# Folding the last heads of a two-layer Hedgehog and Mish kernel in chunks of six, four and four, and making the output weights' parts one by one

## The chip, the cores and the metric

The kernel runs on one core of one Trainium2 chip. The time of a run is the device time in microseconds (us), and lower is better. The engines are called as in the profile: PE is the TensorE's matmuls and PEld its weight loads, DVE the VectorE, ACT the ScalarE, POOL the GpSimd and SP the SyncE, which here only issues DMA.

## The reference

All arrays are float32: x is (1, 2048, 640), wqkv (640, 1920), w_phi (32, 20, 20), wo (640, 640), w1 (640, 1536), w2 (1536, 640). There are 32 heads of 20 columns. The two halves are run twice, with the same weights, so there are two layers.

```
def attention(x, wqkv, w_phi, wo):               # x is layer-normalised
    q, k, v = split per head of x @ wqkv
    pq = q @ w_phi[h];  pk = k @ w_phi[h]        # per head, 20 x 20
    phi_q = concat(softmax(pq), softmax(-pq));  phi_k = the same of pk
    kv = phi_k^T v;  z = sum of phi_k over the sequence
    o = (phi_q @ kv) / (phi_q @ z + 1e-6)
    return concat of heads(o) @ wo

def dense(x, w1, b1, w2):                        # x is layer-normalised
    h = x @ w1 + b1
    return mish(h) @ w2

x = x + attention(norm(x));  x = x + dense(norm(x))
x = x + attention(norm(x));  x = x + dense(norm(x))
```

## The kernel before

**Stages.** Each layer is three stages: `attend_first` (keys, queries and values, and the sum over the sequence), `attend_second` (the averages, the product with wo and the residual) and `dense`. In each the 2048 rows go through in 8 blocks (`NB`) of two tiles (`BT`) of 128 rows, which the text counts from 0. Layer 0's first stage ends at about 263 us of the profiled span; its second and third stages end at about 707, where layer 1 begins.

**Split matmuls.** Every large product is made of three float32r products: each operand is split into a high part (an ACT copy that rounds) and a low part (operand minus high part). So x comes as `xth` and `xtl`, a weight as `r1h`/`r1l` (the wide set of keys and values, later w1) or `r2h`/`r2l` (queries, later wo and w2). `Transposed.step` turns a normalised block on the TensorE (L280), copies it to `xth` on ACT and subtracts on DVE (L286) for `xtl`.

**Folding.** The per-head w_phi is folded into the query and key weights in layer 0 only. The host lays w_phi out as blocks on a diagonal, `phi_bd` (120 x 6 x 120): column group t holds heads 6t to 6t+5, and group 5 holds only heads 30 and 31, 40 rows. `load_raw` fetches the transposed weights wqk_t in the same chunks: five of 120 rows and a sixth of 40. `fold_phi` then makes each of the five 128-row parts `k` of the folded weight in two halves `c`: three matmuls (L237) of float32, one for each chunk, that write side by side into one PSUM tile. The first half covers heads 0 to 17 (360 columns), the second heads 18 to 31 (280 columns: 120, 120 and 40). An ACT copy gives the high part and a DVE subtraction (L243) the low part. The order of the ten halves is that of the tuple in `fold_phi`: first halves of parts 0 to 3, second halves of parts 0 to 3, then both of part 4. The queries are folded at the start, before and among the first projections (L344); the keys at about 36 to 47 us, just before the first key tile of block 0. After block 1 of layer 0 the folded weights are written out (`spill_qk_weights`), and layer 1 reads them back.

**Start.** The first DMAs stand in an order written out by hand (`manual_schedule` for SP, L448 on): the first three groups of `phi_bd`, three query chunks, x of block 0, the other three groups of `phi_bd`, three query chunks, then the weights of the values and the key chunks. The sixth chunk lies in a wide weight tile (`r2_wide`) and the other five in the future places of `r2` tiles.

**Output weights.** wo is made into five parts by the generator `make_five`: at its first step it fetches three parts (L149's raw), and at each later step it makes one part, an ACT copy (L148) and a POOL subtraction (L149), and in the first two of these it fetches one part more. The five fetches land in places of weight tiles not yet used and, the fifth, in a row tile (`row_tile`, a pool of 4 that also holds the normalised rows `xn`). `load_o_weights` runs the whole generator at once, at the end of block 1 of the first stage, in both layers.

**Order.** Within a block of the first stage, `order` gives the sequence of projections (keys, queries, values of the two tiles). Each is a generator: `features` takes a projection through the two softmaxes (reductions, reciprocals and products on DVE and POOL: L368 to L379), and a later step adds its key product to `kva` (L416). The next block's x is fetched and turned in the course of the block. Outside the hand-written part at the start, a scheduler that simulates the timeline sets each engine's order, except that ACT's instructions in `act` and those within `issue_after` keep to a named predecessor. `attend_second` fixes the order of TensorE and SP by hand.

Of the kernel before, what the change touches and what calls it, by code (L numbers as in the profile page):

```python
# [41 lines left out]
def kernel(  # L42
# [77 lines left out]
    def v_tile():  # L120
        return work.tile([P, VW], F32, tag="v", name="v", bufs=2)
# [80 lines left out]
                raws.append(fetch_rows(rows(3 + k), [spares[3 + k]()]))  # L202
            yield w

    def load_o_weights():
        return list(make_five(KD, lambda k: wo[k * P:(k + 1) * P, :]))[1:]

    def w2_pair(f):

        return r2_pair(f if f < 5 else (f + 5 if f < 7 else f - 2))  # L210
# [1 line left out]
    def load_raw(which, ts=range(6)):  # L212

        raw = []
        for t in ts:
            rows = 120 if t < 5 else 40
            if t < 5:
                r = wts.tile([P, D], F32, tag=f"r2{'hl'[which]}{5 + t}", name=f"raw{which}{t}")
            else:
                r = r2_wide(10 + which, F32)[:, 0]  # L220

            n = P if t < 5 else rows
            nc.sync.dma_start(r[:n], wqk_t[which * D + t * 120:which * D + t * 120 + n, :])
            raw.append((r, rows))
        return raw

    def fold_phi(ws, bd, raw):

        pss = {}
        for k, c in ((0, 0), (1, 0), (2, 0), (3, 0), (0, 1), (1, 1), (2, 1), (3, 1), (4, 0), (4, 1)):  # L230
            if c == 0:
                mm = None if k % 2 else mm_tile()
                pss[k] = [one_tile(), one_tile()] if k % 2 else [mm[:, 0], mm[:, 1]]
            ps = pss[k][c]
            for t in range(3 * c, 3 * c + 3):
                r, rows = raw[t]
                nc.tensor.matmul(ps[:, (t % 3) * 120:(t % 3) * 120 + rows],  # L237
                                 r[:rows, k * P:(k + 1) * P], bd[:rows, t, :rows],
                                 start=True, stop=True)
            n0, n1 = (0, 360) if c == 0 else (360, D)  # L240
            hi, lo = ws[k][0][:, n0:n1], ws[k][1][:, n0:n1]
            nc.scalar.activation(hi, ps[:, :n1 - n0], AF.Copy)
            nc.vector.tensor_tensor(lo, ps[:, :n1 - n0], hi.bitcast(F32), op=ALU.subtract)  # L243
# [143 lines left out]
    def attend_first(layer, x_src, first):  # L387


        def fetch_normed(b):  # L390
            if layer:
                return load_turned(n2_d[b], [row_tile] * 3)
            xt = fetch(x_src, b)
            norm_scale(b, [norm_stats(t, xt) for t in range(BT)])
            return xt

        pending = []

        def advance():
            for g in pending[::-1]:  # L400
                try:
                    next(g)
                except StopIteration:
                    pending.remove(g)

        def keys(xts, i, v):
            e = big_tile()
            yield from features(project(xts, i % BT, kv_ws, 0), e, False)
            yield
            if i % BT == 0 and BT < i < NT - BT:  # L410
                yield
            for r in range(9):
                for j in range(4):
                    h = 3 * (4 * (r // 3) + j) + r % 3
                    if h < H:
                        nc.tensor.matmul(kva[32 * j:32 * j + DH + 1, 40 * r:40 * r + 40],  # L416
                                         v[:, (DH + 1) * h:(DH + 1) * (h + 1)], e[:, 40 * h:40 * h + 40],
                                         start=(i == 0 and r == 0), stop=(i == NT - 1), skip_group_check=True)

        def queries(xts, i, ps=None):  # L420
            e = query_tile(i)
            yield from features(project(xts, i % BT, q_ws, 0) if ps is None else ps, e, True)

            nc.vector.transpose(e, e)
            b, t = divmod(i, BT)
            dst = e_d[b].rearrange("(j f) (t q s) -> t q f j s", f=32, t=BT, s=32)
            for q in range(4):
                nc.sync.dma_start(dst[t, q], e[32 * q:32 * q + 32].rearrange("f (j s) -> f j s", s=32))
                if b == NB - 1:
                    yield  # L430

        def values(xts, i, v):
            vv = v.rearrange("p (h d) -> p h d", d=DH + 1)
            act(vv[:, :, DH], ident[:, :H], AF.Copy, scale=0.0, bias=1.0)
            if i < BT:
                pv = project(xts, i, kv_ws, D, [one_tile(), one_tile()])
                for c in range(2):
                    act(vv[:, c * H // 2:(c + 1) * H // 2, :DH],
                        pv[c][:, :HC].rearrange("p (h d) -> p h d", d=DH), AF.Copy)
            else:  # L440
                pv = project(xts, i % BT, kv_ws, D)
                act(vv[:, :, :DH].rearrange("p (c h) d -> p c h d", c=2),
                    both(pv).rearrange("p c (h d) -> p c h d", d=DH), AF.Copy)
            yield

        if first is None:
            with tc.manual_schedule(engines={mybir.EngineType.SP}):
                bd = big_tile()[:120, :720].rearrange("p (t c) -> p t c", t=6)  # L448
                nc.sync.dma_start(bd[:, :3], phi_bd[:, :3])
                raw = load_raw(0, range(3))  # L450
                xt = fetch_normed(0)
                nc.sync.dma_start(bd[:, 3:], phi_bd[:, 3:])
                raw += load_raw(0, range(3, 6))
                nxt = normed(0, xt).all()
                q_ws = [r2_pair(k) for k in range(KD)]
                fold_phi(q_ws, bd, raw)
                kv_ws = load_v_weights()
                raw = load_raw(1)
            nc.sync.dma_start(mask, bass.AP(tensor=head_mask.tensor, offset=head_mask.offset,
                                            ap=[[1, 120], [120 * (DH + 1), 3]]))  # L460
        else:
            nxt, kv_ws = first
            load_k_weights(kv_ws)
            q_ws = load_q_weights()
        for b in range(NB):
            xts = nxt
            order = ("k0", "k1", "v0", "v1", "q0", "q1")
            if b == 0 and layer:
                order = ("v0", "k0", "k1", "v1", "q0", "q1")
            elif b == 0:  # L470
                order = ("v0", "q0", "v1", "k0", "q1", "k1")
            elif b == 1 and not layer:
                order = ("k0", "q0", "k1", "v0", "q1", "v1")
            elif b == NB - 1:
                order = ("k0", "k1", "v0", "v1", "q0")
            vs = [v_tile() for _ in range(BT)]
            for n, (kind, t) in enumerate(order):
                t = int(t)
                i = b * BT + t
                if b == 0 and n == (1 if layer else 3):  # L480
                    if layer == 0:
                        fold_phi(kv_ws, bd, raw)
                    kva = one_tile()
                    nc.vector.memset(kva[:, :360], 0.0)
                if b == NB - 1 and n == 3:
                    loaded = {0: load(0)}
                if b + 1 < NB:
                    if n == 0:
                        xt = fetch_normed(b + 1)
                    elif n == 2:  # L490
                        nxt = xt if layer else normed(b + 1, xt)
                    elif n > 2:
                        nxt.step()
                g = {"k": lambda: keys(xts, i, vs[t]), "q": lambda: queries(xts, i),
                     "v": lambda: values(xts, i, vs[t])}[kind]()
                next(g)
                advance()
                pending.append(g)
            if b == 1:
                if layer == 0:  # L500
                    spill_qk_weights(kv_ws, q_ws)
                o_ws = load_o_weights()

        def rest():

            ps = [one_tile(), one_tile()]
            project_half(ps[0], xts, 1, q_ws, 0, 0)
            advance()
            advance()
            yield  # L510
            project_half(ps[1], xts, 1, q_ws, 0, 1, range(3))
            yield
            project_half(ps[1], xts, 1, q_ws, 0, 1, range(3, KD))
            pending.append(queries(xts, NT - 1, ps))
            next(pending[-1])
            while pending:
                yield
                advance()

        return kva, o_ws, loaded, rest()  # L520
# [374 lines left out]
```

## Time and profile before

| what | value |
|---|---|
| median of 3 runs | 1381.55 us (1381.36 to 1382.13) |
| profiled execution | 1381.04 us, its span 1379.0 |
| granted TensorE clock | 0.999 |
| PE busy | 1364.3 us, 99% |
| DVE busy | 1077.0 us, 78% |
| ACT busy | 583.3 us, 42% |
| POOL busy | 441.0 us, 32% |
| DMA queue of the kernel's transfers | 45.0% of 16 engines' span |

The span is the time from the first to the last instruction of the profiled execution; 2.0 us of the time lie outside of it. A busy share is a sum over the whole span and says little of one stage: in the 40 slices of the page the DMA is at 8 tenths in the first slice and at 2 to 7 later, DVE is at 9 tenths in the third to fifth slice (69 to 172 us, inside layer 0's first stage) and mostly at 6 to 8 elsewhere, and PE is at 9 in all slices but the first, where it has 7, and the last, where it has 8. In a timeline a line gives the start, the length and the engine, then the line of the code, the operation, output and input tiles by their names, their shape, and how many such instructions in a row; idle time before it stands in brackets, with what ended it. Instructions of a row overlap their neighbours, so that the distance of two starts, and not the length, is what one costs.

### The profile page before, as it was taken

To read this page: it belongs to the slowest core of one execution; us is meant where nothing else is said; L and a number is where in the kernel's file an instruction comes from. 1 tells how busy PE (TensorE), PEld (TensorE's weight loads), DVE (VectorE), ACT (ScalarE), POOL (GpSimd) and SP (SyncE) were. 2 spreads that over 40 slices of the span, in tenths; PEclk is the share of its full clock that TensorE was granted. 3 is DMA by queue.
4 is the path that set the end of the run, shared out by engine and by line. 5 is a ranking of instruction groups with operands and counts; after the bars stand their busy time and mean duration, and the time that the engine had idled before them with its cause. 6 is when DMAs were issued, how large, how long until landed. Compare 5 with 4: busy or idle time off the path is not lost.

```text
span 1379.0 us, 30804 instructions
## 1 busy us (share of the span) xinstructions
PE 1364.3 (99%) x12866; PEld 1350.7 (98%) x12866; DVE 1077.0 (78%) x1820; ACT 583.3 (42%) x971; POOL 441.0 (32%) x334
## 2 busy tenths in 40 slices
PE   7999999999999999999999999999999999999998
PEld 7999999999999999999999999999999999999998
DVE  5799977886698887788769898988668776677775
ACT  4444434222355444545454333432235444354443
POOL 1353543353322221222234434453342111111112
PEclk9999999999999999999999999999999999999999
DMA  8532433779624533344473433458965321333200
GB/s 321 173 67 62 73 54 61 211 227 316 227 68 96 115 90 62 80 116 96 117 262 74 95 59 59 70 117 274 297 239 163 77 53 45 97 96 96 77 20 19
DMA packets 350277, 169.67 MB, mean 123 GB/s; under 512 B 287098, under 2 KB 323690, under 8 KB 350138
## 3 DMA queue, kind: packets, MB, share of 16 engines
q1 hardware_dynamic: 350137, 167.72, 45.0%
q8 instruction: 100, 1.64, 0.5%
q14 instruction: 40, 0.32, 0.1%
HBM read 104.76 MB, written 62.91 MB: 122 GB/s over the span
## 4 chain that ended last, share of the span: by engine, by line
PE 94%; DVE 2%; DMA 1%; issue 1%; POOL 0%; SPq 0%; ACT 0%; DVEq 0%; POOLq 0%; ACTq 0%
PE mm L344 26%; PE one L691 24%; PE mm L733 24%; PE one L344 12%; PE mm L569 3%; PE one L280 2%; PE one L416 2%; PE mm L237 1%; DMA raw<-in_wqk_t 1%; DVE m L368 1%; PE one L237 0%; DMA v<-in_wv 0%; DVE big L371 0%; DVE r L377 0%; DMA raw<-in_wo 0%
## 5 line engine op out<-in xcount | busy, mean ns | idle before, releaser
L733 PE MATMUL mm<-r2h,ol 128*128 128x320 f32 x1280 | 305.0, 309 | 0.3 <-ACT ol L716 0.3
L717 POOL TENSOR_TENSOR ol<-big,ol 128x512 fp32r<-128x512 f32 (+1 forms) x98 | 130.4, 1330 | 483.6 <-ACT ol L716 407.4
L691 PE MATMUL one<-xtl,r1h 128*128 128x256 f32 x960 | 268.2, 279 | 0.0
L691 PE MATMUL one<-xth,r1l 128*128 128x256 f32 x960 | 268.0, 279 | 0.0
L691 PE MATMUL one<-xth,r1h 128*128 128x256 f32 x960 | 265.9, 279 | 0.0
L733 PEld LDWEIGHTS mm<-r2h,ol 128*128 128x128 f32 x1280 | 219.2, 188 | 0.6 <-ACT ol L716 0.6
L733 PE MATMUL mm<-r2l,ol 128*128 128x320 f32 x640 | 197.3, 309 | 0.0
L344 PE MATMUL mm<-r1h,xth 128*128 128x320 f32 x600 | 187.5, 312 | 0.0
L344 PE MATMUL mm<-r1h,xtl 128*128 128x320 f32 x600 | 185.8, 310 | 0.4 <-DVE xtl L286 0.4
L344 PE MATMUL mm<-r1l,xth 128*128 128x320 f32 x600 | 186.0, 310 | 0.0
L691 PEld LDWEIGHTS one<-xtl,r1h 128*128 128x128 f32 x960 | 180.4, 188 | 0.0
L691 PEld LDWEIGHTS one<-xth,r1l 128*128 128x128 f32 x960 | 180.4, 188 | 0.0
L691 PEld LDWEIGHTS one<-xth,r1h 128*128 128x128 f32 x960 | 179.6, 188 | 0.0
L706 DVE TENSOR_SCALAR big<-big 128x512 f32<-128x512 f32 (+1 forms) x98 | 56.4, 575 | 110.6 <-ACT big L704 110.4
L379 POOL TENSOR_TENSOR r<-r,r 128x1280 f32<-128x1280 f32 x32 | 76.6, 2395 | 154.3 <-DVE r L378 148.5
L733 PEld LDWEIGHTS mm<-r2l,ol 128*128 128x128 f32 x640 | 120.2, 188 | 0.0
L708 ACT ACTIVATE big<-big,two 128x512 f32<-128x512 f32 (+1 forms) x98 | 70.3, 717 | 116.0 <-DVE big L707 116.0
L704 ACT ACTIVATE big<-one,b1s 128x256 f32<-128x256 f32 x192 | 81.0, 468 | 90.1 <-PE one L691 89.6
L716 ACT ACTIVATE ol<-big 128x512 fp32r<-128x512 f32 (+1 forms) x98 | 61.0, 623 | 136.3 <-DVE big L715 136.2
L344 PEld LDWEIGHTS mm<-r1h,xth 128*128 128x128 f32 x600 | 112.7, 188 | 0.8
L344 PEld LDWEIGHTS mm<-r1h,xtl 128*128 128x128 f32 x600 | 112.7, 188 | 0.7 <-DVE xtl L286 0.6
L344 PEld LDWEIGHTS mm<-r1l,xth 128*128 128x128 f32 x600 | 112.8, 188 | 0.1
(128 smaller groups left out, 3124.0 us busy)
## 6 DMA issues: line engine op xcount, KB each, us to landing
e_d<-r SPq DMA_DIRECT2D x128, 160.0 KB, 4.0
big<-e_d SPq DMA_DIRECT2D x32, 640.0 KB, 7.3
x_d<-xt SPq DMA_DIRECT2D x23, 640.0 KB, 3.6
xt<-x_d SPq DMA_DIRECT2D x22, 640.0 KB, 4.4
n_d<-xn SPq DMA_DIRECT2D x176, 80.0 KB, 2.3
xt<-in_x SPq DMA_DIRECT2D x16, 640.0 KB, 6.8
xn<-x_d SPq DMA_DIRECT2D x28, 320.0 KB, 4.4
v<-n_d SPq DMA_DIRECT2D x30, 256.0 KB, 3.1
```

The source lines that it names most:

```text
L280: nc.tensor.transpose(ps[:, c, t * P:(t + 1) * P], self.rows[t][:, (c0 + c) * P:(c0 + c + 1) * P], ident)
L344: nc.tensor.matmul(ps[:, :HC], a[:, sl], r, start=(k == 0 and n == 0), stop=(k == KD - 1 and n == 2))
L379: nc.gpsimd.tensor_tensor(eg, eg, r.unsqueeze(2).to_broadcast([P, 2 * H, DH]), op=ALU.mult)
L416: nc.tensor.matmul(kva[32 * j:32 * j + DH + 1, 40 * r:40 * r + 40], v[:, (DH + 1) * h:(DH + 1) * (h + 1)], e[:, 40 * h:40 * h + 40], start ...
L569: nc.tensor.matmul(po[64 * q:64 * q + 64, c, GW * j:GW * j + w], phs[g][:n, s0:s0 + 64], kvb[:n, g, :w], start=True, stop=True)
L691: nc.tensor.matmul(ph[:, j, :], l, r, start=(n == 0), stop=(n == 3 * KD - 1))
L704: exps[0] = nc.scalar.activation(part(ta, 0)[:, j - js.start], ph[:, j, :], AF.Exp, bias=b1s[:, 2 * pr + j:2 * pr + j + 1]).ins
L706: nc.vector.tensor_scalar_min(e, e, E_CAP)
L708: nc.scalar.activation(r, n, AF.Ln, bias=two)
L716: nc.scalar.activation(ah[:, js], n, AF.Copy)
L717: nc.gpsimd.tensor_tensor(al[:, js], n, ah[:, js].bitcast(F32), op=ALU.subtract)
L733: nc.tensor.matmul(pys[t][:, c, :HC], l[:, j, sl], r, start=(f == 0 and n == 0), stop=(f == KF - 1 and n == 2))
```

## The change

The last fourteen heads are folded in chunks of six, four and four heads (120, 80 and 80 rows), where they were folded in chunks of six, six and two (120, 120 and 40). For this `phi_bd` stays as it is in memory; group 4 is fetched as before and only its first 80 rows and columns are used, and group 5 is put together in place, from the last two heads of group 4 and the two of group 5, by two DMAs of 40 x 40 elements onto a memset area. The sixth chunk of raw weights is the last 80 rows.

The parts of wo are no longer all made at the end of block 1. There only the three first fetches are issued; one part is then made at the beginning of each of blocks 2 to 6, ordered after the last of ACT's instructions so far. This holds in both layers.

```diff
-    def load_o_weights():
-        return list(make_five(KD, lambda k: wo[k * P:(k + 1) * P, :]))[1:]
...
     def load_raw(which, ts=range(6)):
         for t in ts:
-            rows = 120 if t < 5 else 40
+            rows = 120 if t < 4 else 80
...
             n = P if t < 5 else rows
-            nc.sync.dma_start(r[:n], wqk_t[which * D + t * 120:which * D + t * 120 + n, :])
+            c0 = which * D + (t * 120 if t < 5 else D - rows)
+            nc.sync.dma_start(r[:n], wqk_t[c0:c0 + n, :])
...
     def fold_phi(ws, bd, raw):
...
+            n = 0
             for t in range(3 * c, 3 * c + 3):
                 r, rows = raw[t]
-                nc.tensor.matmul(ps[:, (t % 3) * 120:(t % 3) * 120 + rows],
-                                 r[:rows, k * P:(k + 1) * P], bd[:rows, t, :rows],
+                nc.tensor.matmul(ps[:, n:n + rows], r[:rows, k * P:(k + 1) * P], bd[:rows, t, :rows],
                                  start=True, stop=True)
+                n += rows
...
                 xt = fetch_normed(0)
-                nc.sync.dma_start(bd[:, 3:], phi_bd[:, 3:])
+
+                nc.vector.memset(bd[:80, 5, :80], 0.0)
+                nc.sync.dma_start(bd[:40, 5, :40], phi_bd[80:120, 4, 80:120])
+                nc.sync.dma_start(bd[40:80, 5, 40:80], phi_bd[:40, 5, :40])
+                nc.sync.dma_start(bd[:, 3:5], phi_bd[:, 3:5])
                 raw += load_raw(0, range(3, 6))
...
             vs = [v_tile() for _ in range(BT)]
+            if 2 <= b < 2 + KD:
+                with tc.issue_after(last_act[0]):
+                    o_ws.append(next(o_gen))
...
             if b == 1:
                 if layer == 0:
                     spill_qk_weights(kv_ws, q_ws)
-                o_ws = load_o_weights()
+                o_gen = make_five(KD, lambda k: wo[k * P:(k + 1) * P, :])
+                next(o_gen)
+                o_ws = []
```

## The prediction

> **What bounds the kernel now.** I read the page first, then the waits of the TensorE over the whole span, then the timeline of each place that the diff touches.
>
> ```profile
> PE 1364.3 (99%) x12866; PEld 1350.7 (98%) x12866; DVE 1077.0 (78%) x1820; ACT 583.3 (42%) x971; POOL 441.0 (32%) x334
> ...
> PE 94%; DVE 2%; DMA 1%; issue 1%; POOL 0%; SPq 0%; ACT 0%; DVEq 0%; POOLq 0%; ACTq 0%
> ```
>
> ```profile
> PE mm L237 <- DMA raw<-in_wqk_t: 7.9, 3, 4.4
> ...
> PE mm L344 <- DVE xtl L286: 0.4, 1, 0.4
> ...
> PE mm L237 <- DVE r1l L243: 0.2, 1, 0.2
> ```
>
> The TensorE is busy throughout and the chain that ends last is 94% TensorE. So only two things can save time: TensorE work that goes away, and the few places where it waits. Both lie in layer 0's first stage, up to 91.4 us. Layer 1 folds nothing and has no such wait in its first stage, so there the change can only cost.
>
> Next the timeline of the weight loads in the key folding (columns: start, length from the first to the last end, engine, line, operation, tiles, shape, count). L237 is the folding's matmul, and each of them takes two passes, each with a weight load of its own.
>
> ```profile
> 36.26 0.75 PEld L237 LDWEIGHTS one<-big,raw 120*128 120x128 f32 x6
> 36.93 0.75 PEld L237 LDWEIGHTS mm<-big,raw 120*128 120x128 f32 x6
> 37.60 1.20 PEld L237 LDWEIGHTS one<-big,raw 120*128 120x128 f32 x10
> 38.91 0.29 PEld L237 LDWEIGHTS one<-big,r 40*128 40x128 f32 x2
> 39.25 0.52 PEld L237 LDWEIGHTS one<-big,raw 120*128 120x128 f32 x4
> 39.88 0.29 PEld L237 LDWEIGHTS one<-big,r 40*128 40x128 f32 x2
> 40.23 0.52 PEld L237 LDWEIGHTS mm<-big,raw 120*128 120x128 f32 x4
> ```
>
> Six passes of 120 rows take 0.67 us (36.26 to 36.93). Six passes of which the last two have 40 rows take 0.98 (39.25 to 40.23), though 40 columns fewer go through. The time is lost at the change of row count: four passes to 39.88 take 0.64, not 0.45, and two passes of 40 rows take 0.34, not 0.22. Whether 80 rows are spared this, the same view of the second stage's averages (L569) shows:
>
> ```profile
> 264.40 1.25 PEld L569 LDWEIGHTS mm<-kvb,big 120*64 120x64 f32 x40 [0.19 <-DVE kvb L543]
> 265.56 0.20 PEld L569 LDWEIGHTS mm<-kvb,ol 80*64 80x64 f32 x4
> 265.68 1.25 PEld L569 LDWEIGHTS mm<-kvb,big 120*64 120x64 f32 x40
> ```
>
> 40 loads in 1.16 us and 4 in 0.12 are 0.029 each: going from 120 to 80 rows and back costs nothing.
>
> Last, the two waits that are not DMA, in the timelines of POOL, DVE and the TensorE:
>
> ```profile
> 44.07 1.58 POOL L149 TENSOR_TENSOR r2l<-raw,r2h 128x640 fp32r<-128x640 f32 x1 [0.56 <-PE mm L237]
> ...
> 44.12 1.61 DVE L262 SCALAR_TENSOR_TENSOR stats<-mv,stats 128x1 f32<-128x1 f32 x2
> ...
> 90.95 0.35 DVE L286 TENSOR_TENSOR xtl<-one,xth 128x256 fp32r<-128x256 f32 x1
> ...
> 91.36 0.41 PE L344 MATMUL mm<-r1h,xtl 128*128 128x320 f32 x1 [0.42 <-DVE xtl L286]
> ```
>
> Two tiny DVE instructions (0.23 together at 28.53) take 1.61 while POOL subtracts an output-weight part, and the subtraction behind them (45.65) is what the TensorE waits for at 46.23. At 91.36 it waits for the last split of block 2, out of a DVE that has been busy without a gap since 60.
>
> **Query folding.** Its second halves lose 0.31 each, at 20.39, 22.25 and 25.72; the two earlier ones, whose 40-row passes stand together at 13.32, run at 0.213 per pass and lose about 0.4 in all. That 0.4 is not kept: at 18.84 and 19.75 the TensorE waits for DVE, whose run starts when block 1's x lands (14.29) and reaches the first split at 19.70. That transfer moves. An issue on SP waits for the eighth one before it, and the two added issues put x of block 1 behind block 0's x: it goes out at 9.5, not 6.39. Bytes ahead of it: 102 KB more for 80 rows, 58 less for the band's two groups, 13 for the two small pieces, 57 KB net; at the 297 to 359 GB/s of those slices that is 0.2 us, and queues that run dry until 10.6 may add as much. I take 0.3 later, from 0 (the data queued ahead covers it) to 0.6. Against that, the built order puts the split ahead of two L262 that waited for POOL until 18.84, which is worth 0.37. The third chunk's 120 passes then set the start of the next half near 19.8, 0.1 late; the three later places keep 0.93. **Kept: 0.8** (0.4 to 1.2).
>
> The small issues (SP 0.4 us each) and the memset cost nothing else: the fourth and fifth chunks, issued at 3.54 and 4.29, run only from 7.5 on.
>
> 80-row passes were never timed with 128 columns. 40 rows take 0.108 and 120 rows 0.112, so I use 0.11. The Trainium skill (TensorEngine Tiling, "Theoretical Speedup") speaks against the change here: a contraction of at most 64 rows may run up to twice as fast, which 80 rows would give up. By that page the 20 passes of 40 rows would have cost an estimated 0.055 each, and the gain would shrink by 20 x 0.055 = 1.1 to 1.6. The 0.108 beside 0.112 shows no such speed.
>
> **Key folding.** Four second halves in a row, 38.4 to 42.2: 4 x 0.31 = 1.25. Then the transposes and the fifth chunk's first half, which needs DVE's subtraction for the first (41.90 + 0.44 = 42.34) and starts at 43.33. Its lead of 0.9 to 1.0 is all that can be kept. **Kept: 0.9** (0.5 to 1.25).
>
> **Fifth key chunk.** 0.31 of its own. The wait at 46.23 also goes, as POOL's subtraction is no longer at 44: 0.46 from start to start where 0.15 is normal, 0.31. **Kept: 0.6.**
>
> **Wait at 91.36.** 90.11 to 91.36 holds 64 passes that take 0.75 elsewhere (84.61 to 85.36): 0.5. TensorE arrives 2.3 earlier, DVE too, since its run from 50.75 is started by TensorE. DVE gains more: its L371 at 54.94 takes 1.92 under two of POOL's subtractions and 0.82 without. In the built order block 2's fourth part waits for one POOL multiply sooner, by 11 matmuls or so. **Kept: 0.4** (0 to 0.5).
>
> **The five parts moved.** Each brings 0.72 of ACT, 1.58 of POOL and one DMA issue into blocks 2 to 6 (counted from 0), in both layers. They are free as long as each block's last split is ready before its use: after block 2 the leads are 0.4 us in block 3 (119.55 against 119.93), then 2.5 to 3.8, and in layer 1 1.9 to 2.3. On POOL the multiplies of L379 (2.37) queue behind each, and DVE's transposes wait for those. One row tile stays taken for three blocks; layer 1's loads of the next block then go out a few steps later (783 to 791 instead of up to 22 earlier) and are read from 807. One fetch on SP waits for POOL's first subtraction ahead of block 1's stores (96.71); it ends before them by the rows. **Cost: 0.**
>
> **Sum:** 0.8 + 0.9 + 0.6 + 0.4 = 2.7. The profiled execution took 1381.04 (span 1379.0 and 2.0 around it), 0.5 below the median of 1381.55. 1381.04 - 2.7 = 1378.3 for such an execution, **1378.9** at the median.
>
> **Rivals.**
> *DVE absorbs the folding.* Block 1's x lands 0.6 late and the key folding is bound by DVE's subtractions from its start: 0.4 + 0.3 + 0.6 + 0 = 1.3, so 1380.2. For it: the TensorE's lead over DVE is 0.05 at 19.70. Against: DVE idles 1.5 us before the key folding.
> *Everything is kept.* x lands on time, the earlier split is worth its 0.37, and the key folding keeps all of its 1.25: 0.4 + 0.37 + 8 x 0.31 + 0.3 + 0.5 = 4.05, so 1377.5. For it: none of the five terms is larger than what stands idle or is lost there now. Against: DVE's 42.34.
> *TensorE stays slow longer.* Its passes take 0.213 until 18.2 and 0.111 after, though the granted clock reads 1.00 in both slices. Each us by which the switch comes later loses 0.48 (1 - 0.111/0.213). If it came at 22, after the first new half, 3.8 x 0.48 = 1.8 would go: 1380.7. For it: the new order leaves a gap near 18.7. Against: three runs within 0.8 us, so the switch has not moved about so far. The Trainium skill (TensorE: Matmul & The Clock Gate, "What's actually happening") describes such a gate, which opens after a busy window of 3413 ns; the trace agrees on the factor of two, and a window more would by that page be an estimated 1.6 us.
> *Slower: the moved parts stop the TensorE.* A part's 1.58 on POOL delays the multiply that a DVE transpose waits for, and holds DVE's two-operand work by up to 1.1, 2.7 in all. It decides from the lead: block 3 would lose 2.3, layer 1's five blocks about 0.6 each, layer 0's others 0 to 0.2; 5.5 - 2.7 gives 1384.4. For it: DVE is 88% busy there. Against: moved away from blocks 1 and 2, the same work stops loading DVE where it has no lead.
> That the 80-row chunks do not remove the switch is ruled out by L569.
>
> **How the numbers follow.** 0.2%, about what a measurement of this kernel can tell from no change, is 2.76 us: faster means under 1378.8. The forecast gets 0.50 (its own range 1377.9 to 1379.9, nearly half of it under the bound), everything kept 0.17, DVE 0.17, slow TensorE 0.06, slower 0.10. Faster: 0.23 of the forecast, 0.17, and 0.02 for a DVE case that costs less than worked out: 0.42. Slower: 0.08, the rest of that rival's 0.10 being the cases in which block 3 alone loses its 2.3 (1381.2), which is inside the bound. Same: the remaining 0.50. The range, 1377.4 to 1381.5, takes in the first four with their ends and that milder form of the fifth, with the 0.3 by which the runs of before differ.
>
> **What would show it.** The weight loads of L237 should stand 0.67 apart in second halves, with no step at 80 rows; wrong if 0.98 stays. L262 near 42 should take 0.2; the waits at 46.23 and 91.36 should be gone, and none be new after 92 or in layer 1. The same points of the key stage at 48 should come 2.3 earlier, and the start of layer 1 2.7 earlier. A gain under 1.5 at 48 means that DVE's run from block 1's x decides; a loss between 92 and 262 means the moved parts.

## The result and the profile after

The changed kernel takes 1384.18 us (median of 21 runs, 1382.65 to 1386.96), the kernel before 1382.13 in the same comparison (21 runs, 1379.81 to 1384.55). The ratio is 1.0014, with a 95% interval of 1.0007 to 1.002: it is slower by 2.0 us, where 2.7 less was forecast. The profiled execution took 1382.93, 1.89 more than that of before.

Both traces have 12866 matmuls, so the start of the n-th can be compared with the start of the n-th of before. That places the difference (us, after minus before; the first row is the time in the trace before):

| point | key folding, 46 | layer 0's first stage, 91 | its end, 265 | layer 1, 717 | its block 5, 867 | block 6, 880 | block 7, 908 | stage's end, 932 | last matmul, 1374 |
|---|---|---|---|---|---|---|---|---|---|
| changed kernel | -2.24 | -2.89 | -2.93 | -2.49 | -2.40 | -1.27 | +0.46 | +2.25 | +2.06 |

So layer 0 brought what it should, 2.9 us: about 2 by the folding and about 0.9 by the parts that are no longer made at the waits of 46.23 and 91.36 us (from 43 to 110 us the changed kernel gains 1.0, and fold_only below, in which the parts stay, 0.1). The parts in layer 0's later blocks took nothing of it. Nearly all that was lost, 4.65 us, was lost in the last blocks of layer 1's first stage. The waits of the TensorE over the whole span of the changed kernel show where they go (us in total, times, longest):

```profile
PE mm L343 <- DVE xtl L285: 2.3, 2, 1.5
PE mm L236 <- DVE bn L249: 2.0, 1, 2.0
PE one L415 <- POOL big L378: 1.3, 1, 1.3
```

The second line is at 10.39 us, where the kernel before waited for a DMA. The first and third are new, and in the timeline of the TensorE they stand here:

```profile
875.03 0.41 PE L343 MATMUL mm<-r1h,xtl 128*128 128x320 f32 x1 [0.86 <-DVE xtl L285]
...
904.76 0.41 PE L343 MATMUL mm<-r1h,xtl 128*128 128x320 f32 x1 [1.46 <-DVE xtl L285]
...
930.83 0.83 PE L415 MATMUL one<-big,v 128*21 128x40 f32 x64 [1.28 <-POOL big L378]
```

The TensorE reaches blocks 6 and 7 before the last split of their x is there, and at the end of the stage the last key product waits for POOL's multiply of the last keys.

Another 0.45 us goes between 265 and 717 us, and this is not explained here. Behind the two first stages the traces differ by amounts that do not follow the parts: of the experiments below, fold_only loses 0.7 between 265 and 717, and parts_layer0, whose parts in layer 1 are made as before, loses 0.8 between 932 and 1000. Both stretches hold the DMA's busiest slices in the page of before: 7, 7 and 9 tenths from 241 to 345 us, 8 and 9 from 931 to 1000. (So the DMA's "2 to 7 later", ahead, is too narrow.)

The folding itself, in the weight loads of the key stage after the change (L236 is L237 of before):

```profile
37.62 0.30 PEld L236 LDWEIGHTS one<-big,r 80*128 80x128 f32 x2
37.84 0.53 PEld L236 LDWEIGHTS one<-big,raw 120*128 120x128 f32 x4
38.28 0.30 PEld L236 LDWEIGHTS one<-big,r 80*128 80x128 f32 x2
38.51 0.53 PEld L236 LDWEIGHTS mm<-big,raw 120*128 120x128 f32 x4
...
40.52 0.64 PEld L279 LDWEIGHTS one<-ident,xn 128*128 128x128 f32 x6 [0.24 <-DVE r1l L242]
```

The lines of four hold two passes of 120 rows and two of 80, which the view puts together under the first one's shape. From the sixth chunk of one half (37.62) to that of the next (38.28) it is 0.66 us for six passes, 0.98 before: 0.22 for two passes and 0.44 for four, so no step is left, wherever 120 and 80 rows meet. The last line is the 0.24 that the transposes now wait for DVE's subtractions, which is most of what is not kept of the key folding's gain.

Where the parts go wrong is seen in block 5 of layer 1, the last that the TensorE enters without a wait. First the timelines of DVE and POOL of the kernel before:

```profile
849.59 2.13 DVE L371 TENSOR_TENSOR r<-m,r 128x640 f32<-128x640 f32 x2
...
856.01 0.55 DVE L378 RECIPROCAL r<-r 128x64 f32<-128x64 f32 x1
857.70 1.54 DVE L368 TENSOR_REDUCE m<-big 128x32 f32<-128x640 f32 x2 [1.15 <-ACT big L116]
859.17 0.81 DVE L369 TENSOR_TENSOR big<-big,m 128x640 f32<-128x640 f32 x1
...
849.03 1.28 POOL L369 TENSOR_TENSOR r<-r,m 128x640 f32<-128x640 f32 x1 [1.64 <-DVE m L368]
856.70 2.38 POOL L379 TENSOR_TENSOR r<-r,r 128x1280 f32<-128x1280 f32 x1 [6.39 <-DVE r L378]
```

Then the same work in the changed kernel:

```profile
852.06 0.83 DVE L370 TENSOR_TENSOR r<-m,r 128x640 f32<-128x640 f32 x1 [1.17 <-POOL r L368]
...
857.12 0.55 DVE L377 RECIPROCAL r<-r 128x64 f32<-128x64 f32 x1
857.58 1.48 DVE L367 TENSOR_REDUCE m<-big 128x32 f32<-128x640 f32 x2
858.98 1.88 DVE L368 TENSOR_TENSOR big<-big,m 128x640 f32<-128x640 f32 x1
...
848.64 1.57 POOL L149 TENSOR_TENSOR r2l<-raw,r2h 128x640 fp32r<-128x640 f32 x1 [1.65 <-ACT r2h L148]
850.16 1.87 POOL L368 TENSOR_TENSOR r<-r,m 128x640 f32<-128x640 f32 x1
857.80 2.37 POOL L378 TENSOR_TENSOR r<-r,r 128x1280 f32<-128x1280 f32 x1 [5.78 <-DVE r L377]
```

Read it in order. The part's subtraction (848.64) stands between POOL's two subtractions for the queries, so the second one ends at 852.02, not at 850.31, and DVE waits 1.17 us for it. (It takes 1.87 itself and not 1.28, as DVE's subtraction at 849.43 lies beside it.) From there DVE is 1.1 late (its reciprocal at 857.12, not 856.01). The 1.15 that it used to wait for the second tile's keys would take this up, and it does: the two reductions start at 857.58, even a little earlier than before. But that wait had a use. POOL's multiply starts right behind the reciprocal and lasts 2.37 us; before, it ended at 859.08, just ahead of DVE's key subtraction at 859.17. Now it lasts from 857.80 to 860.17, and the subtraction, begun at 858.98, takes 1.88 us and not 0.81. That is 1.07 us a block, and nothing behind it takes it up: DVE's work on this block begins 0.16 us ahead of the trace before (847.97 against 848.13), and the last split of the next block's x ends 0.89 behind it (874.98 against 874.09).

The Trainium skill (SBUF — State Buffer, "Who interferes with whom") states that a DVE instruction with two SBUF inputs and a GpSimd instruction that reads SBUF exclude each other, and that the later one waits until the first has ended. The trace agrees: the subtraction ends at 860.86, 0.69 behind the multiply's end at 860.17, while the two reductions beside the same multiply, with one input, take their usual 1.5.

### The profile page after: what moved, and what is told of

It is laid out like the page before. It is cut to its first block, busy times and chain, and to the rows that moved or that the text cites. A ratio compares the mean times of both kernels' runs of the same rounds, so it can differ in the third digit from the quotient of the medians.

```text
span 1381.1 us, 30811 instructions
## 1 busy us (share of the span) xinstructions
PE 1363.5 (99%) x12866; PEld 1349.6 (98%) x12866; DVE 1081.9 (78%) x1821; ACT 583.0 (42%) x971; POOL 442.1 (32%) x334
```

## The experiments

Each was timed against the kernel before in the same comparison: 5 runs of parts_only and sub_twice, 11 or 12 of the others, 17 to 27 of the kernel before. The differences behind "Measured" are the ratio and its interval, times the kernel before; 0.1% is 1.4 us.

| kernel | median us | before | ratio, 95% interval |
|---|---|---|---|
| fold_only | 1380.48 | 1382.24 | 0.9987, 0.9979 to 0.9996 |
| parts_only | 1386.55 | 1382.24 | 1.0031, 1.0019 to 1.0044 |
| parts_layer0 | 1379.79 | 1382.24 | 0.9981, 0.9972 to 0.9990 |
| parts_later | 1379.69 | 1382.24 | 0.9979, 0.9970 to 0.9987 |
| low_on_act | 1380.02 | 1381.95 | 0.9987, 0.9978 to 0.9996 |
| sub_twice | 1389.94 | 1381.95 | 1.0059, 1.0046 to 1.0071 |
| low_on_dve | 1382.88 | 1381.95 | 1.0009, 1.0000 to 1.0018 |
| parts_three | 1381.86 | 1381.95 | 0.9999, 0.9991 to 1.0008 |
| one_early | 1378.99 | 1381.98 | 0.9978, 0.9970 to 0.9987 |
| one_late | 1380.82 | 1381.98 | 0.9989, 0.9980 to 0.9998 |
| one_middle | 1381.02 | 1382.10 | 0.9993, 0.9984 to 1.0001 |

The second table is what the traces say of layer 1: the TensorE's lead, that is, the start of its first matmul with the last split of a block's x less the end of that split on DVE, and how long the second key subtraction takes on DVE. A lead of 0.05 is a wait.

| kernel | lead at blocks 3, 4, 5, 6, 7 | second key subtraction in blocks 3 to 7 |
|---|---|---|
| before | 1.90, 2.31, 2.15, 2.32, 2.31 | 0.82, 0.97, 0.81, 0.82, 0.82 |
| after | 1.88, 1.04, 0.11, 0.05, 0.05 | 1.88, 1.88, 1.88, 1.89, 1.87 |
| parts_later | 1.88, 2.22, 2.02, 2.32, 2.32 | 0.91, 1.11, 0.81, 0.82, 0.81 |
| sub_twice | 1.49, 0.05, 0.05, 0.06, 0.05 | 1.87, 1.88, 1.87, 1.88, 1.03 |
| low_on_dve | 1.89, 1.47, 0.59, 0.07, 0.05 | 1.67, 1.87, 1.88, 1.87, 1.87 |
| parts_three | 1.90, 0.78, 0.05, 0.37, 0.05 | 1.88, 1.87, 1.88, 1.87, 1.87 |
| one_early | 1.89, 2.32, 2.04, 2.25, 2.31 | 0.82, 1.09, 0.87, 0.81, 0.81 |
| one_middle | 1.90, 0.77, 0.86, 1.10, 0.62 | 1.89, 1.87, 1.88, 1.87, 1.87 |
| one_late | 1.88, 2.09, 1.82, 2.02, 0.53 | 1.04, 1.30, 1.11, 1.88, 1.87 |

### Which half of the change, which layer, which place

**fold_only.** `load_o_weights` and its call are put back.

```diff
-            if 2 <= b < 2 + KD:
-                with tc.issue_after(last_act[0]):
-                    o_ws.append(next(o_gen))
...
-                o_gen = make_five(KD, lambda k: wo[k * P:(k + 1) * P, :])
-                next(o_gen)
-                o_ws = []
+                o_ws = load_o_weights()
```

> The chunks of six, four and four alone; the output weights' parts are all made at the end of block 1 in both layers, as before. Theory A (the five moved parts lengthen the period of layer 1's first stage on DVE and POOL by about 1.0 us a block, so that the lead of 2.3 us is used up): layer 1 is as before, its first stage has no wait over 0.5 us; of the 2.94 us that the changed kernel had gained at 92 us, the 0.31 at 46.23 and about 0.2 of the 0.5 at 91.36 stay lost; 2.3 us faster than before. Rival B (the TensorE arrives 2.4 us earlier in layer 1, and the other engines can't follow, whatever the parts do): layer 1 loses about as much as the TensorE gained, 0 to 2 us slower than before.

Measured: 1.8 us faster (0.6 to 2.9). The two waits of 0.4 us in layer 0, near 46 and 91, stay. No wait in layer 1's first stage, and the leads there are those of before (1.88, 2.25, 1.97, 2.22, 2.31). That speaks against rival B, but weakly: in this trace the TensorE enters layer 1 only 0.7 ahead of the trace before. In parts_layer0 and parts_later, below, it enters 2.2 and 2.1 ahead and loses nothing in the stage, and there rival B falls: an earlier TensorE alone does not outrun the other engines.

**parts_only.** The three hunks on wo alone, on the kernel before.

```diff
+            if 2 <= b < 2 + KD:
+                with tc.issue_after(last_act[0]):
+                    o_ws.append(next(o_gen))
```

> The parts one by one in blocks 2 to 6, in both layers; the chunks as before. Theory A: the same three waits in layer 1 as in the changed kernel (1.0, 1.7 and 1.5 to 1.8 us), 0.5 us gained in layer 0: 4 us slower than before. Rival B: as the folding is that of before, no wait in layer 1; 0.5 us faster than before.

Measured: 4.3 us slower (2.6 to 6.1). Its leads are 1.89, 0.65, 0.05, 0.06 and 0.05, and it gains 0.3 in layer 0 across the place of the wait at 91.36. The loss comes with the parts, without the new chunks: 5.1 us in this trace between 717 and 932.

**parts_layer0.**

```diff
-            if 2 <= b < 2 + KD:
+            if not layer and 2 <= b < 2 + KD:
...
+                if layer:
+                    o_ws = list(o_gen)[1:]
...
```

> The chunks of six, four and four, and the parts one by one in layer 0 only; in layer 1 they are all made at the end of block 1, as before. Theory A: the gain of 2.4 us that stands at the start of layer 1 is kept: 2.4 us faster than before. Rival B: the waits of layer 1 stay: 2 us slower than before.

Measured: 2.6 us faster (1.4 to 3.9). The five parts cost in layer 1 only.

**parts_later.** In layer 1 the part is made at the third step of the block.

```diff
-            if 2 <= b < 2 + KD:
-                with tc.issue_after(last_act[0]):
-                    o_ws.append(next(o_gen))
             for n, (kind, t) in enumerate(order):
                 t = int(t)
                 i = b * BT + t
+                if 2 <= b < 2 + KD and n == (2 if layer else 0):
+                    with tc.issue_after(last_act[0]):
+                        o_ws.append(next(o_gen))
```

> As the changed kernel, but in layer 1 each part is made ahead of the third step of its block, not the first, so that POOL subtracts it behind both of the queries' subtractions and not between them. Theory A in its narrow form (DVE waits 1.15 us a block for POOL's second subtraction of the queries, which the part pushes back): the period of DVE's splits in layer 1 goes from 29.0 to 28.0, no wait over 0.5 us; 2.4 us faster than before. Rival C (it is not the place on POOL but the work itself, the copy on ACT, the port that POOL and DVE share, or the row tile that stays taken): as the changed kernel, 2 us slower than before.

Measured: 2.9 us faster (1.8 to 4.1). All parts are still in the same blocks, with the same copies, subtractions, fetches and row tile; only the step of the block differs, for ACT's copy as for POOL's subtraction. The timelines of DVE and POOL, again in block 5:

```profile
855.65 1.54 DVE L367 TENSOR_REDUCE m<-big 128x32 f32<-128x640 f32 x2 [1.05 <-ACT big L116]
857.12 0.81 DVE L368 TENSOR_TENSOR big<-big,m 128x640 f32<-128x640 f32 x1
...
854.75 2.37 POOL L378 TENSOR_TENSOR r<-r,r 128x1280 f32<-128x1280 f32 x1 [6.34 <-DVE r L377]
857.48 1.88 POOL L149 TENSOR_TENSOR r2l<-raw,r2h 128x640 fp32r<-128x640 f32 x1 [0.36 <-ACT r2h L148]
```

DVE waits 1.05 for the keys again, the multiply ends at 857.12 as the subtraction starts, and this time it is the part that waits for DVE (1.88 us, not 1.57), where nobody waits for it. Rival C falls: the same work costs nothing at another place.

### What it is about the place

**low_on_act.** In layer 1 the kernel leaves out POOL's subtraction: the low part is a second copy on ACT, which is not the value that the product needs, so this kernel serves for its time alone.

```diff
+            if low is None:
+                nc.scalar.activation(w[1][:, cs], st, AF.Copy)
+            else:
...
-                o_gen = make_five(KD, lambda k: wo[k * P:(k + 1) * P, :])
+                o_gen = make_five(KD, lambda k: wo[k * P:(k + 1) * P, :], None if layer else nc.gpsimd)
```

> As the changed kernel, but in layer 1 the low part of wo is a second copy on ACT in place of POOL's subtraction (so the low part holds another value); copy, fetches, row tile and blocks stay. Theory A in its narrow form (POOL's subtraction stands between the two subtractions of the queries): POOL's place is free, so the splits of layer 1 keep a period of 28.0 us and the TensorE waits nowhere for over 0.5 us there; 2.4 us faster than before. Rival C (ACT's copies, the late fetches or the row tile that stays taken): ACT has 0.7 us more a block, so the waits stay or grow; 2 us or more slower than before.

Measured: 1.8 us faster (0.6 to 3.0), leads of 1.90, 2.22, 1.95, 2.14 and 2.32. With nothing on POOL the place is harmless, though ACT does more. As ACT's first copy stays at the block's first step here, it is POOL's subtraction and not the copy whose place counts.

**sub_twice.**

```diff
-            low.tensor_tensor(w[1][:, cs], st, w[0][:, cs].bitcast(F32), op=ALU.subtract)
+            for _ in range(twice):
+                low.tensor_tensor(w[1][:, cs], st, w[0][:, cs].bitcast(F32), op=ALU.subtract)
...
+                o_gen = make_five(KD, lambda k: wo[k * P:(k + 1) * P, :], twice=1 + layer)
```

> As the changed kernel, but in layer 1 POOL does each part's subtraction twice; in the built order the second one stands behind the second subtraction of the queries, where POOL idles for 5 us now. Theory A, narrow (what costs is the place between the two): 1.58 us more on POOL a block cost nothing; 2 us slower than before, as the changed kernel. Theory A, wide (POOL's work in the block is what costs, 1.0 us for 1.58): the period grows by another 1.0 to 1.6 us a block; 7 to 10 us slower than before.

Measured: 8.2 us slower (6.4 to 9.8). The narrow form, which I held, is wrong, and the timelines of DVE and POOL show why:

```profile
855.41 2.18 DVE L371 TENSOR_TENSOR r<-m,r 128x640 f32<-128x640 f32 x1 [1.17 <-POOL r L369]
...
853.52 1.85 POOL L369 TENSOR_TENSOR r<-r,m 128x640 f32<-128x640 f32 x1
855.34 1.57 POOL L150 TENSOR_TENSOR r2l<-raw,r2h 128x640 fp32r<-128x640 f32 x1
```

POOL does idle there, but DVE does not: its own second subtraction, released by the same event, meets the extra one and takes 2.18, not 0.83 as in the changed kernel. So it is not POOL's queue alone. The wide form gets the size and not the reason: parts_later has the changed kernel's POOL work and no loss, so what counts is which of DVE's two-input instructions a POOL instruction falls on.

**low_on_dve.** `make_five` gets `nc.vector` for layer 1.

```diff
-                o_gen = make_five(KD, lambda k: wo[k * P:(k + 1) * P, :])
+                o_gen = make_five(KD, lambda k: wo[k * P:(k + 1) * P, :], nc.vector if layer else nc.gpsimd)
```

> As the changed kernel, but in layer 1 DVE subtracts the part, not POOL; in the built order it stands between the two subtractions of the queries' minima, where DVE waits for POOL in the changed kernel. If POOL alone is to blame: 2.4 us faster than before. If it is enough that DVE reaches the later key subtraction late (in the changed kernel POOL's multiply of 2.37 us, pushed back by 1.1 us with it, falls on that subtraction and stretches it from 0.81 to 1.88 us): DVE is 0.8 us late there by its own work, the multiply moves as far, and most of the loss stays: 0 to 2 us slower than before.

Measured: 1.2 us slower (0 to 2.5). POOL has no part to do in layer 1's first stage, DVE 0.81 us more, and the key subtraction is still met by the multiply, as the timelines of DVE and POOL show:

```profile
850.48 0.81 DVE L149 TENSOR_TENSOR r2l<-raw,r2h 128x640 fp32r<-128x640 f32 x1
...
858.13 1.88 DVE L368 TENSOR_TENSOR big<-big,m 128x640 f32<-128x640 f32 x1
...
856.95 2.37 POOL L378 TENSOR_TENSOR r<-r,r 128x1280 f32<-128x1280 f32 x1 [7.08 <-DVE r L377]
```

From the block's first reduction to the reciprocal it is 8.57 us here (847.70 to 856.27) and 7.88 before (848.13 to 856.01). So a lateness of 0.7 us that comes from DVE's own work is enough as well. The price then comes from the multiply.

### Does the lateness heal?

**parts_three.** Two parts at the end of block 1, three in blocks 2 to 4.

```diff
-            if 2 <= b < 2 + KD:
+            if 2 <= b < 2 + KD - 2 * layer:
...
-                o_ws = []
+                o_ws = [next(o_gen) for _ in range(2 * layer)]
```

> As the changed kernel, but in layer 1 two of the parts are made at the end of block 1 and three in blocks 2 to 4. Theory A says that each part takes 0.9 to 1.1 us off a lead of about 2.9 us in the changed kernel, and that the TensorE waits only when the lead is used up: the leads of the last split fall to about 1.9, 1.0 and 0.1 us and then recover, with no wait over 0.3 us; 2.4 us faster than before. A cost that is paid part by part (a fifth of 4.5 us each): 0.3 us slower than before.

Measured: as before, 0.1 us faster (1.2 faster to 1.1 slower). Theory A said that the lead recovers when no part comes. It doesn't: blocks 5 to 7 have no part, their key subtractions take 1.88, 1.87 and 1.87 all the same, and 1.6 us are lost at the end of the stage (-1.40 at 908, +0.19 at 932). Another 1.2 go behind it, where parts_layer0 loses 0.8 too, so these are not put down to the parts. This gave theory D.

**one_early.** Four parts at the end of block 1, one in block 2.

```diff
-            if 2 <= b < 2 + KD:
+            if (b == 2 if layer else 2 <= b < 2 + KD):
...
-                o_ws = []
+                o_ws = [next(o_gen) for _ in range(4 * layer)]
```

> As the changed kernel, but in layer 1 four parts are made at the end of block 1 and a single one in block 2. Theory D (a single push is enough: DVE's wait of 1.1 us for the second tile's keys is what keeps POOL's multiply of 2.37 us clear of the key subtraction; once DVE is 1 us late the two overlap, the subtraction takes 1.87 us in place of 0.82 in every later block, part or not, and the lateness stays until the stage ends, where the TensorE has no lead and pays it): the second key subtraction takes 1.8 to 1.9 us in all of blocks 2 to 7; the TensorE loses 1.5 to 2.7 us, most of it at the end of the stage and behind it; 0 to 0.9 us faster than before. Theory A as first put (each part costs 1 us of a lead that grows back): 0.81 to 0.9 us again from block 3 on; 2.4 us faster than before.

Measured: 3.0 us faster (1.8 to 4.1), with subtractions of 0.81 to 1.09. As theory D put it, this was wrong. In block 2 DVE has a second wait: 0.67 us for POOL and then 1.18 for the first tile's keys (764 and 766 us, read in the trace of one_middle, which has no part there). In one_early it waits 1.85 for POOL and then not at all for those keys, which is the sum of the two:

```profile
764.98 0.82 DVE L370 TENSOR_TENSOR r<-m,r 128x640 f32<-128x640 f32 x1 [1.85 <-POOL r L368]
765.90 1.55 DVE L367 TENSOR_REDUCE m<-big 128x32 f32<-128x640 f32 x2
```

The push was taken up ahead of the place where it hurts. So one_early did not test whether lateness stays; the next two do.

**one_late** and **one_middle.** The same with `b == 6` and `b == 3`.

> As the changed kernel, but in layer 1 four parts are made at the end of block 1 and the last one in block 6. Theory D: the second key subtraction takes 0.8 to 1.2 us up to block 5 and 1.8 to 1.9 in blocks 6 and 7; no wait of the TensorE inside the stage, since the lead of 2.3 us covers it, but the lateness is paid at its end, 1.0 to 2.3 us; 0.1 to 1.4 us faster than before. Theory A as first put: one part takes 1 us off a lead of 2.3, so nothing is lost; 2.4 us faster than before.

Measured: 1.5 us faster (0.3 to 2.8). Subtractions of 1.04 to 1.30 up to block 5, 1.88 and 1.87 in blocks 6 and 7, no wait of the TensorE in layer 1 up to 908 us, 1.4 us lost from there to the end of the stage. The time alone does not decide between theory D (0.1 to 1.4) and theory A (2.4); the stretched subtractions and the loss at the end of the stage do.

> As the changed kernel, but in layer 1 four parts are made at the end of block 1 and the last one in block 3, where DVE has no other wait in front of the second tile's keys that could take the push up (in block 2 it had one). Theory D (one push is enough, and the lateness stays): the second key subtraction takes 0.8 to 1.2 us in blocks 1 and 2 and 1.8 to 1.9 in each of blocks 3 to 7, of which only block 3 has a part; the TensorE waits less than 1 us inside the stage and 1 to 2 us at its end; 0 to 1.4 us faster than before. Theory A as first put (the lead grows back when no part comes): 0.8 to 1.2 us again from block 4 on, no wait at the end; 2.4 us faster than before.

Measured: 1.0 us faster (0.1 slower to 2.2 faster). The one part is in block 3, and from there on all five blocks have 1.87 to 1.89. The timelines of DVE and POOL for block 6, three blocks behind the part:

```profile
877.08 2.12 DVE L370 TENSOR_TENSOR r<-m,r 128x640 f32<-128x640 f32 x2
...
883.45 0.54 DVE L377 RECIPROCAL r<-r 128x64 f32<-128x64 f32 x1
883.91 1.47 DVE L367 TENSOR_REDUCE m<-big 128x32 f32<-128x640 f32 x2
885.31 1.87 DVE L368 TENSOR_TENSOR big<-big,m 128x640 f32<-128x640 f32 x1
...
884.13 2.37 POOL L378 TENSOR_TENSOR r<-r,r 128x1280 f32<-128x1280 f32 x1 [6.34 <-DVE r L377]
```

No part is near and DVE waits neither for POOL nor for the keys; because it is late it does not wait, because it does not wait it meets the multiply, and that keeps it late. Leads stay at 0.6 to 1.1, so the TensorE waits nowhere inside the stage; it loses 1.3 us at its end (-2.49 at 908, -1.17 at 932). Theory D holds for blocks 3 to 7. No run takes the multiply itself away or shortens it, so that the meeting keeps up the lateness is read from the traces.

What stays open is the way by which lateness comes back to DVE in the next block. In both kernels DVE's first instruction of a block waits for ACT's copy of the second queries (1.88 us before, 2.12 after), and ACT for the stores of an earlier query tile (ACT waits on those 29.3 us in layer 1's first stage before and 38.6 after). These stores come behind DVE's transposes, so a circle through the two query tiles is likely, but a third query tile was not tried.

## Why the prediction was wrong, step by step

- **Query folding**, 0.8: held in size, with luck in it. The trace is 1.08 ahead from 26 us on, but the eleven traces with the new chunks range from 1.08 ahead to 1.47 behind there, with 0.73 ahead in the middle: the start alone varies by more than this term. Block 1's x did not come 0.3 later, as the term had it; DVE's statistics of it start at 13.83, and at 14.29 before.
- **Key folding**, 0.9: held. The four halves bring 1.2 (1.08 to 2.26 ahead between 26.06 and 42.18), and the wait of the transposes for DVE takes 0.3 back, as worked out: 1.93 ahead at the fifth chunk's first matmul.
- **Fifth key chunk**, 0.6: 0.7 (1.93 to 2.64). L261 near 42 takes 0.23 and the wait at 46.23 is gone.
- **Wait at 91.36**, 0.4: 0.3, and it is gone.
- **The five parts moved, "Cost: 0"**: this is the step that failed. Sum without it: 2.94 at 110 us, against 2.7. With it, layer 1 lost 4.65. The step compared each block with its own lead, 1.9 to 2.3 us in layer 1. But the lead is one stock for the whole stage: the TensorE takes 28.0 us a block there, DVE with a part 28.9 to 29.1 (last splits at 788.07, 816.92, 845.85, 874.98), and the lead goes 1.88, 1.04, 0.11, then waits. In layer 0 the TensorE, which turns x itself, takes 29.1 a block (the mean of four), and DVE with a part 27.9 to 29.1; nothing was lost there, as forecast (-2.94 at 110 us, -2.93 at 265).
- That step named POOL's multiplies and the transposes that wait for them, but not DVE's idle 1.15 us a block ahead of the second tile's keys. It takes up the delay, as read above, but it also kept DVE's two-input subtraction clear of POOL's multiply. And the end of the stage has no lead at all; I had only looked at the splits.
- **"Slower: the moved parts stop the TensorE"**, 1384.4 at a chance of 0.10: this is the rival that came, at 1384.18. Its size was nearly right (5.5 lost, 4.65 measured), its places were not: block 3 of layer 0 lost nothing of the 2.3 it was given, and layer 1 lost 4.65 and not about 3. That the time agrees to 0.2 us is luck: two errors of opposite sign, and a kernel before that took 0.6 us more in this comparison than in the one forecast from (2.8 slower by the rival, 2.0 measured). It also named both prices, the delay of POOL's multiply and the hold on DVE's two-operand work. What spoke "against" it, that the parts leave a place where DVE has no lead, was true of layer 0 (0.3 gained at 91.36) and said nothing of layer 1.
- The other rivals: the TensorE's passes still fall to 0.11 before 19 us, and DVE did not bind the folding beyond the 0.24 us for which the transposes wait. That 80 rows would be slower per column is refuted: 0.11 a pass.

What was forecast for the whole change, 2.7 us, is what parts_layer0 and parts_later measure, which have no loss in layer 1's first stage: 2.6 and 2.9 us faster than before. These two and one_early beat both kernels.

## What to carry to other kernels

A lead that is the same in every block is a balance and not a reserve per block: work added to each block is paid out of one stock, so compare the period of the helping engine with that of the bounding one, add up over the stage, and ask what stands at its end. An idle gap on DVE may be what keeps two instructions apart; before counting it as cover, shift the engine by the gap and see which POOL instruction then lies on which two-input DVE instruction. And place added POOL work where DVE does reductions or waits for another engine, not ahead of something that DVE waits for: here the same five subtractions cost 4.65 us at a block's first step and nothing at its third.

## What the runs showed of the hardware that was not expected

One push of about 1 us in block 3 changed the key subtraction from 0.82 to 1.87 us in that block and the four behind it, without any further push (one_middle): two orders of the same instructions, one in step and one not, both hold themselves. And the step from 120 to 40 rows that cost 0.31 us in a second half has no counterpart from 120 to 80 (0.66 for six passes against 0.98).
